# Pinning the sums of keys and values of batches 2 to 7 behind their neighbour in VectorE's queue

## The chip, the cores and the metric

The kernel runs on one core of one Trainium2 chip. The metric is the device time of one execution in microseconds (us). A core has a matrix engine (TensorE, PE in the profile, with its weight loads as PEld), VectorE (DVE), ScalarE (ACT), GpSimd (POOL) and SyncE (SP), whose queue issues the transfers between HBM and on-chip memory. Each engine has an instruction queue of its own.

## The reference

An attention with pooled keys and values feeds a dense feed-forward layer, whose output feeds a routed layer of eight experts. Cut to what matters here:

```python
# q, k, v: (8 batches, 8 heads, 576 tokens, 64)
k_p = k.reshape(B, H, 72, 8, D).mean(axis=3)      # mean over 8 neighbouring tokens
v_p = v.reshape(B, H, 72, 8, D).mean(axis=3)
attn = softmax(q @ k_p.transpose(0, 1, 3, 2) / sqrt(64))
x = (attn @ v_p) laid out as (4608 tokens, 512)
x2 = softplus(x @ w_in) @ w_out                   # 512 -> 2048 -> 512
out = top expert of 8 for each row of x2, weighted by its softmax probability
```

The change concerns how the means over 8 tokens (kept as sums; the factor is taken care of elsewhere) are placed among the other work.

## The kernel before

**Tiling.** The 4608 tokens are 12 blocks of 384. For each block the dense layer runs over 16 slices of the hidden width (`fc` 0 to 15): `mm1` makes a slice of the hidden layer on TensorE, `softplus` turns it on ScalarE and VectorE into `g`, `split_wo` prepares the second weights (ScalarE, then GpSimd or VectorE), and `mm2`, which trails `mm1` by two slices, adds into the block's four sums in PSUM. At a block's end `x2_out` copies the sums (ScalarE and VectorE) and stores them to HBM.

**Attention between the slices.** Block 0 and the attention that it needs are given first, by a list written out by hand (`ORDER`). From block 1 on there are two gaps per slice (lines 1033 to 1045), and `make_plan` (line 447) hands each gap its steps of attention: loading and transposing a tile of queries (`Q`), its scores and softmax (`S`), the transposes of the weights (`T`), the products with the values (`AV`), and the preparation of keys and values of batches 2 to 7. Of each such batch the plan gives, in this order: `FK`, the copies of keys from HBM (two of 512 KB, one of 128 KB); at least nine gaps later seven `PK` pieces (five sums of keys, `ks` four times and `klm` once, then two multiplications `km` on GpSimd, line 201); four `KT` pieces (the transposes of `km` and `klm` on TensorE, lines 252 and 255, and two copies to `kbd` on VectorE, lines 257 and 260); after the `PK` pieces `FV`, the copies of values (two of 512 KB and six of 64 KB); at least nine gaps later four `PV` and two `PR` pieces (six sums of values, `vs` four times and `vl` twice). `build_r` and `build_v` (lines 278 to 299) take the sums of values up when the previous batch's last `AV` is given.

**Buffers.** The copies of keys and values of these batches go into three buffers (pool `stp`, tag `st`). `FK` needs the buffers that the sums of values of the batch before have read, and `FV` those that the sums of keys of its own batch have read. All copies are issued from SP's queue.

**What sets the order.** TensorE's and SP's instructions stand in their queues as the program gives them (`manual_schedule`, line 997). For VectorE, ScalarE and GpSimd, behind the hand-written part, the compiler's scheduler chooses the order by a simulated timeline: an instruction whose inputs are there in that timeline may be placed ahead of ones given earlier.

**The sums.** A sum is one `tensor_reduce` over a 128 x 512 (or 96 x 512, 64 x 512) tile on VectorE: `pool_sum`, line 173, called by `add` (line 193) from `prep_k`, `prep_v` and `prep_r`. Steps named in `ALT` use three additions on GpSimd in its place; all of those belong to batches 0 and 1. The time-line and wait rows below name the sums by line 173, TensorE's scores by line 322, its second transposes of attention by line 393, its hidden layer and sums by lines 629 to 631, the router's product by line 709.

Of the kernel before, what the change touches and what calls it, by code (L numbers as in the profile page):

```python
# [13 lines left out]
ALU = mybir.AluOpType  # L14
AX = mybir.AxisListType
# [5 lines left out]
def tile_attention_moe_moe(  # L21
# [13 lines left out]
    nc = tc.nc  # L35
    P = 128
    B, H, S, D = q.shape
    POOL = 8
# [130 lines left out]
            nc.sync.dma_start(qt[p0:p0 + n], q[b, :, s:s + n, :].rearrange("h s d -> s h d"))  # L169
        q_t[t] = qt  # L170

    def pool_sum(dst, src):
        nc.vector.tensor_reduce(dst, src.rearrange("p (e d) -> p d e", e=POOL), AX.X, ALU.add)

    def rows(a, b):
        return a[b].rearrange("h (s e) d -> (h s) (e d)", e=POOL)
# [7 lines left out]
    def tree_sum(dst, src):  # L184
        nc.gpsimd.tensor_tensor(src[:, 0:4 * D], src[:, 0:4 * D], src[:, 4 * D:], ALU.add)
        nc.gpsimd.tensor_tensor(src[:, 0:2 * D], src[:, 0:2 * D], src[:, 2 * D:4 * D], ALU.add)
        nc.gpsimd.tensor_tensor(dst, src[:, 0:D], src[:, D:2 * D], ALU.add)


    def alt(step):  # L190
        return step in ALT

    def add(dst, src, step):
        (tree_sum if alt(step) else pool_sum)(dst, src)


    def times(dst, src, by, b, eng):
# [36 lines left out]
    def prep_k(b):  # L234
        ks = kp.tile([P, NJ, D], F32, tag="ks", name=f"ks{b}")
        for j in range(NJ):
            add(ks[:, j, :], st_t["k", b, j // 2][:, j % 2, :], f"K{b}.s{j}")
            yield
        add(klm[:, 1, :], st_t["kl", b][0:64, :], f"K{b}.s4")
        yield  # L240
        km = tp.tile([P, NJ, 2, D], F32, tag="wf", bufs=2, name=f"km{b}")
        km_t[b] = km
        for hh in range(2):
            times(km[:, :, hh, :], ks, hm[:, hh:hh + 1], b, "V" if alt(f"K{b}.m{hh}") != (hh == 1) else "A")
            yield
# [18 lines left out]
    def prep_v(b):  # L264
        vs = kp.tile([P, NJ, D], F32, tag="vs", name=f"vs{b}")
        kv_t[b] = vs
        for j in range(NJ):
            add(vs[:, j, :], st_t["v", b, j // 2][:, j % 2, :], f"V{b}.s{j}")
            yield
# [842 lines left out]
```

## Time and profile before

| | |
|---|---|
| median of three runs | 1480.05 us (1479.39 to 1480.74) |
| the profiled execution | 1478.74 us, its span 1476.9 us |
| TensorE busy over the span | 1396.5 us (95%) |
| VectorE, ScalarE, GpSimd busy | 781.4, 741.5, 330.0 us |
| mean granted clock of TensorE | 0.977 of full speed |
| sums by line 173 | 75, of 1.0 to 1.1 us each |

All times inside a run are microseconds from the start of the span of the profiled execution. A row of a time line gives the start, the duration, the engine, the line, the operation, what is written and read with its sizes, and in square brackets how long the engine was idle before it and what ended that. Durations of the queue's own instructions (SPq) are those of issuing, not of the transfer.

### The profile page before, as it was taken

How to read it: one execution, taken by the hardware profiler on the slowest of the kernel's cores; microseconds unless marked ns; L12 is line 12 of the kernel's file. 1: busy time of each engine (PE TensorE's matmuls, PEld its weight loads, DVE VectorE, ACT ScalarE, POOL GpSimd, SP SyncE). 2: the span in 40 equal slices, each digit the busy share in tenths (PEclk: the TensorE clock that was granted, in tenths of full speed). 3: DMA queues.
4: the chain of work that ended last, by engine and by line, in shares of the span. 5: the costliest groups of instructions: out<-in, count | busy, mean ns of one | idle time of the engine just before them, and what ended most of it. 6: DMA issues, size and time to landing. Idle time of an engine off the chain costs nothing.

```text
span 1476.9 us, 20327 instructions
## 1 busy us (share of the span) xinstructions
PE 1396.5 (95%) x7810; PEld 1315.9 (89%) x7810; DVE 781.4 (53%) x1599; ACT 741.5 (50%) x1593; POOL 330.0 (22%) x305
## 2 busy tenths in 40 slices
PE   5778989899988999998899999999999999999998
PEld 5667979798988999898899999999989999999997
DVE  6989876677566566656556564645513111111111
ACT  4776756466664666666466666767621111111111
POOL 5853432223122131312222121214200000000000
PEclk8889999999998999999999999999999999999999
DMA  7552411113021030302102010105123211111101
GB/s 236 182 167 72 144 39 47 58 47 97 8 83 47 1 97 8 97 8 82 47 1 65 1 51 1 43 1 185 58 107 87 85 65 64 65 64 65 64 22 44
DMA packets 71379, 99.92 MB, mean 68 GB/s; under 512 B 40040, under 2 KB 50280, under 8 KB 68208
## 3 DMA queue, kind: packets, MB, share of 16 engines
q1 hardware_dynamic: 71280, 98.60, 20.4%
q8 instruction: 63, 1.03, 0.3%
q14 instruction: 36, 0.29, 0.1%
HBM read 70.27 MB, written 28.31 MB: 67 GB/s over the span
## 4 chain that ended last, share of the span: by engine, by line
PE 75%; DVE 10%; DMA 7%; ACT 3%; SPq 2%; issue 1%; POOL 1%; DVEq 0%; ACTq 0%; POOLq 0%
PE h L629 11%; PE h L631 11%; PE h L630 11%; PE acc L629 7%; PE acc L631 7%; PE acc L630 7%; PE y L630 5%; PE y L631 5%; DMA st<-in_v_dram 5%; PE y L629 4%; PE pp L322 2%; DMA q<-in_q_dram 1%; DVE g L661 1%; SPq L230 1%; PE lg L709 1%
## 5 line engine op out<-in xcount | busy, mean ns | idle before, releaser
L629 PE MATMUL h<-xT,wi 128*128 128x384 f32 x768 | 265.7, 346 | 6.6 <-DVE t L657 5.9
L630 PE MATMUL h<-xT,wi 128*128 128x384 f32 x768 | 260.2, 339 | 2.2 <-DVE xT L431 2.1
L629 PE MATMUL acc<-g,wo 128*128 128x384 f32 x748 | 259.0, 346 | 2.8 <-ACT sq L699 2.8
L631 PE MATMUL h<-xT,wi 128*128 128x384 f32 x768 | 259.8, 338 | 0.0
L630 PE MATMUL acc<-g,wo 128*128 128x384 f32 x748 | 251.8, 337 | 0.8 <-DVE g L661 0.8
L631 PE MATMUL acc<-g,wo 128*128 128x384 f32 x748 | 252.0, 337 | 0.0
L621 POOL TENSOR_TENSOR wo<-wof,wo 128x512 fp32r<-128x512 f32 x95 | 125.0, 1316 | 443.5 <-ACT wo L617 443.4
L826 DVE SCALAR_TENSOR_TENSOR h<-h,h 128x384 fp32r<-128x384 f32 x96 | 53.5, 557 | 311.1 <-ACT h L825 311.1
L825 ACT ACTIVATE h<-h 128x384 fp32r<-128x384 f32 x96 | 47.2, 492 | 323.5 <-PE h L631 323.5
L661 DVE TENSOR_TENSOR g<-t,g 128x384 fp32r<-128x384 f32 x187 | 146.7, 784 | 51.0 <-ACT g L659 50.3
L657 DVE SCALAR_TENSOR_TENSOR t<-h,t 128x384 f32<-128x384 f32 x187 | 103.5, 553 | 132.0 <-ACT t L649 130.0
L645 ACT ACTIVATE t<-h 128x384 f32<-128x384 f32 x192 | 94.0, 490 | 147.4 <-PE h L631 146.8
L629 PEld LDWEIGHTS h<-xT,wi 128*128 128x128 f32 x768 | 146.8, 191 | 9.2 <-DVE t L657 6.8
L617 ACT CAST wo<-wof 128x512 fp32r<-128x512 f32 x187 | 116.2, 621 | 72.0 <-PE acc L631 69.7
L630 PEld LDWEIGHTS h<-xT,wi 128*128 128x128 f32 x768 | 146.6, 191 | 3.4 <-DVE xT L431 3.1
L629 PEld LDWEIGHTS acc<-g,wo 128*128 128x128 f32 x748 | 141.5, 189 | 7.7 <-ACT sq L699 5.7
L631 PEld LDWEIGHTS h<-xT,wi 128*128 128x128 f32 x768 | 146.4, 191 | 0.0
L630 PEld LDWEIGHTS acc<-g,wo 128*128 128x128 f32 x748 | 141.5, 189 | 1.6 <-DVE g L661 1.3
L631 PEld LDWEIGHTS acc<-g,wo 128*128 128x128 f32 x748 | 141.3, 189 | 0.0
L659 ACT CAST g<-t 128x384 fp32r<-128x384 f32 x187 | 96.0, 513 | 73.9 <-DVE t L657 73.4
L631 PE MATMUL h<-x2T,w 128*128 128x384 f32 x384 | 129.5, 337 | 0.0
L629 PE MATMUL h<-x2T,w 128*128 128x384 f32 x384 | 129.3, 337 | 0.0
(193 smaller groups left out, 2485.2 us busy)
## 6 DMA issues: line engine op xcount, KB each, us to landing
x2s<-x SPq DMA_DIRECT2D x12, 1536.0 KB
x2T<-x2s SPq DMA_DIRECT2D x12, 1536.0 KB
out_dram<-o SPq DMA_DIRECT2D x36, 256.0 KB
st<-in_k_dram SPq DMA_DIRECT2D x16, 512.0 KB
q<-in_q_dram SPq DMA_DIRECT2D x32, 256.0 KB
st<-in_v_dram SPq DMA_DIRECT2D x16, 512.0 KB
st<-in_moe_w_in_dram SPq DMA_DIRECT2D x16, 512.0 KB
st<-in_moe_w_out_dram SPq DMA_DIRECT2D x16, 512.0 KB
```

The lines of the kernel that those rows point to most:

```text
L322: nc.tensor.matmul(pp[p0:p0 + n, i, :], qT[:, j, p0:p0 + n], kbd_t[b][:, j, :], start=True, stop=True)
L617: nc.scalar.copy(w[:, 0, :], wof[:, fc, :])
L621: eng.tensor_tensor(w[:, 1, :], wof[:, fc, :], f32(w)[:, 0, :], ALU.subtract)
L629: nc.tensor.matmul(ps, ll, rh, start=first, stop=False)
L630: nc.tensor.matmul(ps, lh, rl, start=False, stop=False)
L631: nc.tensor.matmul(ps, lh, rh, start=False, stop=last)
L645: nc.scalar.activation(t, h, AF.Abs)
L657: nc.vector.scalar_tensor_tensor(t, h, 0.0, t, ALU.max, ALU.add)
L659: nc.scalar.copy(g[:, 0, :], t)
L661: nc.vector.tensor_tensor(g[:, 1, :], t, f32(g)[:, 0, :], ALU.subtract)
L825: nc.scalar.activation(g[:, 0, :], h, AF.Relu)
L826: nc.vector.scalar_tensor_tensor(g[:, 1, :], h, 0.0, f32(g)[:, 0, :], ALU.max, ALU.subtract)
```

## The change

`pool_sum` takes a third argument. For batches 2 to 7 it is true, and the sum is handed to `keep_in_program_order`, which adds one edge of order, without a wait for completion, from the instruction that was given last on the same engine to the sum. The sum can then not be placed ahead of that one instruction. Nothing keeps that neighbour from being moved, and instructions given after the sum may still be placed ahead of it. `add` reads the batch's number out of the step's name ("K5.s2" is batch 5). Instructions, sizes, buffers and the program's own order are the same.

```diff
-    def pool_sum(dst, src):
-        nc.vector.tensor_reduce(dst, src.rearrange("p (e d) -> p d e", e=POOL), AX.X, ALU.add)
+    def pool_sum(dst, src, pin):
+        ins = nc.vector.tensor_reduce(dst, src.rearrange("p (e d) -> p d e", e=POOL), AX.X, ALU.add)
+        if pin:
+            tc.keep_in_program_order(ins)
...
     def add(dst, src, step):
-        (tree_sum if alt(step) else pool_sum)(dst, src)
+        if alt(step):
+            tree_sum(dst, src)
+        else:
+            pool_sum(dst, src, int(step[1:step.index(".")]) > 1)
```

## Rows read from the trace of the kernel before

**Rows 1.** The page's first part: busy time of each engine, share of the span, instructions.

```profile
PE 1396.5 (95%) x7810; PEld 1315.9 (89%) x7810; DVE 781.4 (53%) x1599; ACT 741.5 (50%) x1593; POOL 330.0 (22%) x305
```

**Rows 2.** The waits of TensorE between 150 and 1000 us: what waited, for what, us in total, times, longest; the two largest.

```profile
PE pp L322 <- DVE aL L399: 10.6, 2, 5.4
PE pl L393 <- DVE xT L431: 9.0, 3, 4.8
```

**Rows 3.** TensorE's time line at its eight idle times of over 1 us between 150 and 1000 us.

```profile
190.12 0.85 PE L709 MATMUL lg<-x,eT 128*32 128x384 f32 x2 [3.68 <-DVE kbd L257]
...
273.52 0.85 PE L322 MATMUL pp<-kbd,qT 128*128 128x144 f32 x2 [5.69 <-DVE kbd L257]
...
364.75 0.44 PE L629 MATMUL h<-xT,wi 128*128 128x384 f32 x1 [1.97 <-DVE t L657]
...
441.43 0.42 PE L393 MATMUL pl<-ident,el 128*96 128x128 f32 x2 [3.73 <-DVE xT L431]
...
476.09 1.33 PE L322 MATMUL pp<-kbd,qT 128*128 128x144 f32 x4 [5.45 <-DVE aL L399]
...
618.11 0.45 PE L629 MATMUL h<-xT,wi 128*128 128x384 f32 x1 [2.10 <-DVE t L657]
...
695.87 0.66 PE L393 MATMUL pl<-ident,el 128*96 128x128 f32 x2 [4.83 <-DVE xT L431]
...
731.45 0.85 PE L322 MATMUL pp<-kbd,qT 128*128 128x144 f32 x2 [5.16 <-DVE aL L399]
```

**Rows 4.** Windows at the six stretches of lower clock between 150 and 1000 us, and one of the same length right behind one of them: the stretch, its length, then busy time and count of PE, PEld, DVE, ACT and POOL, the granted clock, the share of the DMA engines, GB/s.

```profile
189.94:193.35 3.41, 3.23 (x11) 1.78 (x12) 3.41 (x8) 1.95 (x4) 2.08 (x1) 0.50 0.12 37
271.86:278.69 6.83, 5.17 (x17) 4.74 (x17) 4.90 (x10) 1.61 (x3) 2.66 (x3) 0.50 0.00 1
442.53:445.94 3.41, 3.41 (x13) 3.41 (x12) 1.95 (x5) 1.55 (x3) 0.12 (x1) 0.50 0.02 5
473.25:480.08 6.83, 3.99 (x14) 4.00 (x15) 5.20 (x10) 0.51 (x1) 1.18 (x2) 0.50 0.01 4
695.11:701.94 6.83, 6.07 (x20) 6.06 (x21) 3.81 (x8) 1.91 (x4) 1.95 (x3) 0.50 0.00 0
729.25:736.08 6.83, 4.63 (x16) 4.64 (x17) 5.20 (x10) 0.51 (x1) 1.18 (x2) 0.50 0.00 0
480.08:483.49 3.41, 3.41 (x21) 3.41 (x21) 0.99 (x3) 2.01 (x5) 0.00 (x0) 1.00 0.00 0
```

**Rows 5.** Windows with line 173 alone: the stretch, its length, VectorE's busy time in sums and their count, clock, DMA share, GB/s. The first holds the sums of values of batch 5, the second the sums of keys of batch 6.

```profile
466.00:476.00 10.00, 6.12 (x6) 0.86 0.11 42
545.00:552.00 7.00, 5.27 (x5) 1.00 0.29 106
```

**Rows 6.** VectorE's time line in two of the bursts of sums (keys of batch 5, values of batch 5), and, in the last two rows, the view of line 173: us and times that VectorE sat idle ahead of a sum until a copy landed, over the whole run.

```profile
440.03 1.01 DVE L173 TENSOR_REDUCE klm<-st 64x64 f32<-64x512 f32 x1
440.97 0.41 DVE L431 TENSOR_TENSOR xT<-pv,xT 128x256 fp32r<-128x256 f32 x1
...
466.11 1.07 DVE L173 TENSOR_REDUCE vs<-st 128x64 f32<-128x512 f32 x1 [2.13 <-DMA st<-in_v_dram]
...
474.43 1.01 DVE L173 TENSOR_REDUCE vl<-st 96x64 f32<-96x512 f32 x1 [2.27 <-DMA st<-in_v_dram]
475.35 0.68 DVE L399 TENSOR_TENSOR aL<-pm,aH 128x512 fp32r<-128x512 f32 x1
...
  DMA st<-in_v_dram: 18.0, 9
  DMA st<-in_k_dram: 6.6, 5
```

**Rows 7.** VectorE's time line at five instructions that the program gives right ahead of a sum: of the third and fourth sum of keys of batch 2, of the fourth of batch 3, of the second of batch 5, of the last (`klm`) of batch 5, and of the first sum of values of batch 5.

```profile
174.41 0.69 DVE L621 TENSOR_TENSOR wo<-wof,wo 128x512 fp32r<-128x512 f32 x1
...
255.74 0.42 DVE L431 TENSOR_TENSOR xT<-pv,xT 128x256 fp32r<-128x256 f32 x1 [0.41 <-ACT xT L429]
...
479.16 0.55 DVE L661 TENSOR_TENSOR g<-t,g 128x384 fp32r<-128x384 f32 x1
...
489.31 0.55 DVE L661 TENSOR_TENSOR g<-t,g 128x384 fp32r<-128x384 f32 x1
...
519.76 0.68 DVE L621 TENSOR_TENSOR wo<-wof,wo 128x512 fp32r<-128x512 f32 x1
```

**Rows 8.** TensorE's time line at the first transposes of the keys of batches 2, 3 and 5 (line 252), and, last, the view of line 201: the multiplications of keys on GpSimd, with least, median and greatest duration in ns, first and last start.

```profile
180.78 0.60 PE L252 MATMUL pk<-ident,km 128*128 128x128 f32 x4
...
266.74 0.49 PE L252 MATMUL pk<-ident,km 128*128 128x128 f32 x3
...
507.21 0.38 PE L252 MATMUL pk<-ident,km 128*128 128x128 f32 x2
...
L201 POOL TENSOR_SCALAR km<-ks,hm x12: 922/960/1438, 156.6 to 695.2; 128x256 f32<-128x256 f32 x12
```

**Rows 9.** Transfers. SP's time line at the six small copies of values of batch 5 (one row for the six); then two pieces of the chain of work that ended last, in order of time (start, us, what): the landing of the last of these copies, and that of a tile of queries; then TensorE's time line at the tile of queries whose load stands in SP's queue right behind the copies of values of batch 2.

```profile
462.19 3.99 SPq L230 DMA_DIRECT2D st<-in_v_dram  x6
...
465.58 8.77 DMA st<-in_v_dram
...
167.83 9.42 DMA q<-in_q_dram
...
230.32 0.49 PE L305 MATMUL pq<-ident,q 128*128 128x128 f32 x3
```

## The prediction

> **What bounds the kernel now.** I read the page's busy times first. TensorE is busy 95% of the span, VectorE 53% [rows 1], so TensorE sets the end, and what can be won is its idle time and its time at a lower clock. Next the waits of TensorE, between 150 and 1000 us, where the pinned sums lie: the largest end at VectorE [rows 2]. Its time line then gives the places: eight idle times of 3.68, 5.69, 1.97, 3.73, 5.45, 2.10, 4.83 and 5.16 us, 32.6 us together [rows 3]. The next question is what VectorE was doing just before each. Values of batch 5 show it: six sums stand in one burst, 6.1 us of work in 10 us [rows 5], the queue stands still 2.13 and 2.27 us for copies that have not landed, and the aL that TensorE waits for starts only when the last sum is out of the way, at 475.35 [rows 6]; TensorE starts at 476.09. With keys of batch 5 the same: the sums end at 441.0, and xT, which TensorE wants at 441.43, starts at 440.97 [rows 3, 6]. In the other six the sequence is the same: a burst of line 173 ends, what TensorE waits for follows it. So the sums were placed far ahead of their turn, in one run each, and the queue behind them pays.
>
> The last view is the granted clock. [...] At 0.50 it gets through 13 instructions in 3.41 us of full work, at 1.00 through 21, close to half [rows 4].
>
> **The change part by part.** It removes and adds no instruction. It moves 66 sums (five of keys and six of values in each of six batches) back behind the instruction given just ahead of each.
>
> *How far they move.* Each neighbour can be found in the trace by counting the instructions of its line. The second sum of keys of batch 5 has its neighbour at 479.16 and klm at 489.31 [rows 7], where today the burst ends with klm at 440.03 [rows 6]; the first sum of values of batch 5, today at 466.11, has it at 519.76 [rows 6, 7]. So these move some 50 us back, and the plan's pieces put one or two sums in a gap and not six in a run.
>
> *What goes away: waits of VectorE for copies.* VectorE idles 18.0 us for values and 6.6 us for keys ahead of sums over the run [rows 6]. With the moved sums a copy must land later to be late. The last six copies of values of batch 5 could be issued only when klm has been summed (their buffer): 489.31 + 0.55 + 1.05 = 490.9; six issues take 3.99 us and the last lands 8.77 us after its issue [rows 7, 9], so all is there by 503.7, and the first sum stands behind 519.76. 16 us are spare, and I put these waits at nothing from batch 2 on.
>
> *What goes away: idle time of TensorE.* All eight idle times end behind a burst [rows 3], so I take off the whole 32.6 us.
>
> *What goes away: the lower clock.* A stretch at 0.50 costs half of the time that TensorE works in it. Of the six, it works 3.23, 5.17, 3.41, 3.99, 6.07 and 4.63 us [rows 4], together 26.5, so 13.2 us come back if no idle time takes their place.
>
> *What it may add: keys too late.* The transposes of keys stand in TensorE's queue, which waits in order, so a late sum stops it. Batch 2 is tightest: the neighbour ends at 175.1, two sums (2.1 us) and two multiplications on GpSimd (0.96 each) give 179.1, the transposes come at 180.78 [rows 7, 8]: 1.7 us spare. Batch 3: 256.2 + 1.05 + 1.9 = 259.1 against 266.74, 7.6 us spare; batch 5: the fourth sum has the same neighbour as the third, an instruction before 479.16, so the multiplications end by about 484 against 507.21 [rows 7, 8]. Bounds for batch 2: nothing, or about 2 us if its klm, behind a chain of other work, comes a sum late. I take 0.5 us.
>
> *What it may add: SP's queue.* The copies of values now wait for the last sum of keys at its later place, and the loads of queries queue behind them. In batch 2 the last sum of keys stands close to the transposes at 180.78 [rows 8]; with some microseconds of delay and 4 us of issues the copies are out by about 190, the next tile of queries lands 9.42 us after its issue, near 200, and TensorE wants it at 230.32 [rows 9]. I put this at nothing; with that cover gone it would cost what the load is late.
>
> *What it may add: each sum delays its surroundings by 1.05 us.* 66 sums make 70 us, all at new places. The nearest row: the five sums of keys of batch 6 in a burst, with 5.27 us of work at 545 to 552 [rows 5], are followed by no idle time of TensorE [rows 3]. If five in a row pass unseen, one or two mostly will too. The lower bound is a small gain (VectorE has less in front of it elsewhere), say -1.5 us; the upper, if one sum in three met a deadline with no slack, is 22 x 1.05 = 23 us. I take 3 us, near the lower end, because of that row.
>
> *What is late next.* With the eight gone, TensorE's own work is the limit: in the stretch right behind the burst of batch 5 it is busy 3.41 of 3.41 us at full clock [rows 4].
>
> The sum, against the profiled execution: 1478.74 - 32.6 - 13.2 + 0.5 + 3 = 1436.4. The median of the runs lies 1.31 us above the profiled one, so 1437.7, rounded to 1438.
>
> **The rivals.**
>
> *Half comes back (chance 0.18).* The sums sit at better places, but where a gap holds two of them beside attention steps, VectorE still hands over late, and some idle times of 3 us or more pull the clock down again. For it: 70 us of sums must go somewhere, and the aL or xT that TensorE waits for has little slack [rows 3]. Against it: the burst of batch 6 [rows 5]. Half of 45.8 us: about 1457.
>
> *Nothing comes of it (0.05).* The edge binds a sum to one neighbour alone. If the scheduler moves the neighbours forward as well, the bursts stay, and the time stays at 1480. Against it: such neighbours, an xT behind ScalarE by 0.41 us, a wo, a g [rows 7], have inputs that are not there early. The same time would follow if busy shares decided: VectorE is busy 53% [rows 1], so relief on it would be worth nothing. [...] The rows do not bear that reading out here: TensorE's idle times end at VectorE [rows 2].
>
> *Slower (0.07).* A pinned sum now waits for its copy with all of VectorE behind it. The place is the ring of three buffers: values are fetched when the keys' sums are done, the next keys when the values' sums are done, both now later. Its price from the burst of batch 5: VectorE held 4.4 us by two waits and 6.1 us by sums cost TensorE 5.45 us [rows 3, 5, 6], so about 5 us of a hold pass unseen. If each of the 12 groups held VectorE 10 us, TensorE would lose 5 us twelve times and 2.2 us of clock each time (13.2 over six), 86 us against the 45.8 won: about 1520. It decides from some 7 us of hold per group on, at which copies would have to land over 20 us later than I reckon, given the 16 us spare. [...]
>
> **How the numbers follow.** The forecast has 0.70, half back 0.18, nothing 0.05, slower 0.07. The lower end is the sum with no cost for late keys and the -1.5 us: 1478.74 - 45.8 - 1.5 + 1.31 = 1432.8; a microsecond more for the spread of runs, 1431. The upper end takes in most of the half-back case, 1458; what lies above it is about 0.2. Faster by over 0.2% (3 us, about what a measurement of this kernel can tell from no change): 0.88, within it 0.05, slower 0.07.
>
> **What would show it.** In the changed kernel's time line the sums stand singly or in pairs, those of values of batch 5 behind a time of about 510 us; idle ahead of line 173 for copies is near nothing after 150 us; the eight idle times of TensorE are gone and its clock stays at 1.00 from 150 to 1000 us. The first 145 us and everything from the experts on stay as they are. The prediction is wrong if TensorE's waits at lines 252 or 255 (late keys), at 305 (late queries) or at 322 and 393 (VectorE late again) appear in their place.

## The result and the profile after

The changed kernel takes 1431.08 us (median of four, 1430.42 to 1431.41) against 1479.72 for the kernel before on the same chip: a ratio of 0.967, 95% interval 0.966 to 0.969, or 48.6 us. The span of the profiled execution falls from 1476.9 to 1429.7 us. In the rows below the lines of the changed kernel count seven higher than before (the scores are line 329, aL 406, xT 438); the sum is line 175.

The page's first part and its row of the granted clock, which answer to [rows 1]:

```profile
PE 1384.9 (97%) x7810; PEld 1307.8 (91%) x7810; DVE 783.3 (55%) x1599; ACT 743.6 (52%) x1593; POOL 330.5 (23%) x305
...
PEclk8889999999999999999999999999999999999999
```

VectorE's busy time is as before (783.3 against 781.4 us). TensorE is idle for 1429.7 - 1384.9 = 44.8 us where it was idle for 80.4, which is 35.6 us less, and its own work takes 11.6 us less, since less of it runs at the lower clock (mean granted clock 0.977 before, 0.986 after). The two make up the 47.2 us of the span. The same two between 150 and 1000 us, in the window view of each kernel (columns as in [rows 4]), first before, then after:

```profile
150.00:1000.00 850.00, 813.24 (x4823) 790.07 (x4822) 534.03 (x1128) 530.41 (x1154) 215.78 (x187) 0.98 0.15 46
```

```profile
150.00:1000.00 850.00, 845.87 (x5089) 824.15 (x5088) 563.57 (x1180) 567.87 (x1227) 235.25 (x202) 1.00 0.19 57
```

The idle time, the length less PE's busy time, has gone from 36.8 to 4.1 us, and the clock is 1.00 throughout. All that is left of TensorE's waits there, against [rows 2]:

```profile
PE acc L636 <- ACT sq L706: 2.4, 6, 0.6
PE pl L400 <- DVE xT L438: 0.6, 1, 0.6
PE pp L329 <- DVE kbd L264: 0.3, 1, 0.3
PE pk L262 <- DVE kbd L264: 0.2, 1, 0.2
```

Of the eight places of [rows 3] one is left, with 0.29 us in place of 5.69: the scores that wait for kbd at batch 3. VectorE's time line shows where the six sums of values of batch 5 stand now, against the burst of [rows 5, 6]:

```profile
490.51 0.68 DVE L628 TENSOR_TENSOR wo<-wof,wo 128x512 fp32r<-128x512 f32 x1
491.11 1.09 DVE L175 TENSOR_REDUCE vs<-st 128x64 f32<-128x512 f32 x1
...
498.91 1.07 DVE L175 TENSOR_REDUCE vs<-st 128x64 f32<-128x512 f32 x1
...
500.97 1.07 DVE L175 TENSOR_REDUCE vs<-st 128x64 f32<-128x512 f32 x1
...
509.35 1.07 DVE L175 TENSOR_REDUCE vl<-st 96x64 f32<-96x512 f32 x1
...
510.81 1.07 DVE L175 TENSOR_REDUCE vs<-st 128x64 f32<-128x512 f32 x1
511.81 1.05 DVE L175 TENSOR_REDUCE vl<-st 96x64 f32<-96x512 f32 x1
```

The reader is to see three things: the first sum stands right behind its neighbour wo, the six are spread over 22 us and not 9, and no bracket tells of a wait for a copy. The view of line 175 says the same for the whole run; the 3.0 us left lie in the first 12 us, and the wait for values has no row any more:

```profile
  DMA st<-in_k_dram: 3.0, 3
```

### The profile page after: what moved, and what is told of

Its sections match the earlier page's. It is cut to its first block, busy times and chain, and to the rows that moved or that the text cites. A ratio compares the mean times of both kernels' runs of the same rounds, so it can differ in the third digit from the quotient of the medians.

```text
span 1429.7 us, 20346 instructions
## 1 busy us (share of the span) xinstructions
PE 1384.9 (97%) x7810; PEld 1307.8 (91%) x7810; DVE 783.3 (55%) x1599; ACT 743.6 (52%) x1593; POOL 330.5 (23%) x305
## 4 chain that ended last, share of the span: by engine, by line
PE 84%; DVE 8%; ACT 3%; DMA 2%; issue 1%; POOL 1%; SPq 0%; DVEq 0%; ACTq 0%; POOLq 0%
PE h L636 13%; PE h L638 13%; PE h L637 13%; PE acc L636 8%; PE acc L637 8%; PE acc L638 8%; PE y L637 5%; PE y L638 5%; PE y L636 5%; PE pp L329 2%; DVE g L668 1%; PE lg L716 1%; DMA q<-in_q_dram 1%; PE pq L312 1%; DVE wof L614 1%
## 5 line engine op out<-in xcount | busy, mean ns | idle before, releaser
L832 ACT ACTIVATE h<-h 128x384 fp32r<-128x384 f32 x96 | 47.2, 492 | 323.5 <-PE h L638 323.5
L636 PEld LDWEIGHTS h<-xT,wi 128*128 128x128 f32 x768 | 144.8, 189 | 3.8 <-DVE t L664 2.1
L637 PEld LDWEIGHTS h<-xT,wi 128*128 128x128 f32 x768 | 144.7, 188 | 2.6 <-DVE xT L438 2.3
L638 PEld LDWEIGHTS h<-xT,wi 128*128 128x128 f32 x768 | 144.4, 188 | 0.0
L638 PE MATMUL h<-x2T,w 128*128 128x384 f32 x384 | 129.5, 337 | 0.0
L636 PE MATMUL h<-x2T,w 128*128 128x384 f32 x384 | 129.3, 337 | 0.0
L637 PE MATMUL h<-x2T,w 128*128 128x384 f32 x384 | 128.9, 336 | 0.0
```

The costliest lines, as they stand in the source:

```text
L636: nc.tensor.matmul(ps, ll, rh, start=first, stop=False)
L637: nc.tensor.matmul(ps, lh, rl, start=False, stop=False)
L638: nc.tensor.matmul(ps, lh, rh, start=False, stop=last)
L832: nc.scalar.activation(g[:, 0, :], h, AF.Relu)
```

## The experiments

Each was timed in three rounds beside the kernel before on the same chip (1477.8 to 1480.1 us there); the ratios are to that kernel. Where a run is set against the changed kernel, the two medians can come from different chips, on which the kernel before alone differs by 2.3 us; a difference of that size says nothing.

**Keys alone, values alone.** The condition in `add` asks for one kind of sum as well.

```diff
-            pool_sum(dst, src, int(step[1:step.index(".")]) > 1)
+            pool_sum(dst, src, int(step[1:step.index(".")]) > 1 and step[0] == "K")    # run 1
+            pool_sum(dst, src, int(step[1:step.index(".")]) > 1 and step[0] != "K")    # run 2
```

> Only the 30 sums of keys of batches 2 to 7 are pinned; the 36 sums of values may float. Theory A (a burst of early sums holds VectorE by its waits for copies and by its own work together; TensorE pays what goes beyond some 5 us, and half of the time that it then works at the lower clock): the bursts of values stay, and with them idle times of about 24 us and 8.5 us of clock, so about 1431 + 32 = 1463 us (1452 to 1470). Theory B (only VectorE's waits for copies cost, not the work in the burst): values carry 18.0 of 24.6 us of those waits, so about 1431 + 0.75 x 49 = 1467. Theory C (the gain comes from copies being issued at other times): keys' pins alone delay the copies of values, so most of the gain is there, 1435 to 1445.

> Only the 36 sums of values are pinned; the sums of keys may float. Theory A: the two bursts of keys that stopped TensorE (batches 5 and 7: 3.73 and 4.83 us, and 4.7 us of clock) stay, about 1431 + 13 = 1444 us (1436 to 1448). Theory B: keys carry 6.6 of 24.6 us of the waits, about 1431 + 13 = 1444 as well; but the idle times would follow the waits, so batch 6 (2.75 us of wait) would stop TensorE before batch 5 (none). Theory C: the copies of keys come later, those of values do not, so about half of the gain, 1455.

Keys alone: 1470.98 us, ratio 0.994 (0.992 to 0.996). Values alone: 1454.36 us, 0.983 (0.981 to 0.986). The first speaks against theory C: the pins of keys alone bring little, though they delay the copies of values. The second came out at C's 1455, so C is taken up again below. Both runs lie above theory A's ranges, by 1 and 6 us, and the two gains, 9 and 25 us, don't add up to 48.6. With keys alone the values' idle times moved and grew. VectorE's time line in batch 4 of that run:

```profile
369.46 2.05 DVE L175 TENSOR_REDUCE vs<-st 128x64 f32<-128x512 f32 x2
373.34 1.01 DVE L175 TENSOR_REDUCE vl<-st 96x64 f32<-96x512 f32 x1 [1.83 <-DMA st<-in_v_dram]
...
377.11 1.01 DVE L175 TENSOR_REDUCE vl<-st 96x64 f32<-96x512 f32 x1 [2.30 <-DMA st<-in_v_dram]
...
379.67 0.29 DVE L438 TENSOR_TENSOR xT<-pv,xT 128x128 fp32r<-128x128 f32 x1 [0.33 <-ACT xT L436]
```

TensorE's time line, where it takes that xT up:

```profile
380.11 0.60 PE L421 MATMUL pv<-aH,VL 128*128 128x320 f32 x1 [6.57 <-DVE xT L438]
```

The floating sums of values now run into the pinned sums of keys and then wait for copies that were issued later than before: the six small ones of batch 4 at 366.64, right behind its first two sums of values (364.56 to 366.62), where it was 348.64, 7 us ahead of the burst. VectorE's wait for values is 23.8 us in all, where it was 18.0. With values alone the two idle times of keys stood where theory A had them, batches 5 and 7:

```profile
431.96 0.66 PE L400 MATMUL pl<-ident,el 128*96 128x128 f32 x2 [3.77 <-DVE xT L438]
...
678.60 0.66 PE L400 MATMUL pl<-ident,el 128*96 128x128 f32 x2 [4.86 <-DVE xT L438]
```

Batch 6 has none, though its first sum of keys waited 3.09 us for its copy (2.75 in the kernel before). So for keys the wait is not what counts. Two more idle times, of 2.20 and 1.86 us, came up at 215 and 316 us, where floating sums of keys stand between the pinned sums of values of the batch before; they are part of what lies above theory A's range.

**Short sums, floating.** In the kernel before:

```diff
-        nc.vector.tensor_reduce(dst, src.rearrange("p (e d) -> p d e", e=POOL), AX.X, ALU.add)
+        nc.vector.tensor_reduce(dst, src[:, 0:n * D].rearrange("p (e d) -> p d e", e=n), AX.X, ALU.add)
...
+            pool_sum(dst, src, 1 if int(step[1:step.index(".")]) > 1 else POOL)
```

> The kernel before with nothing pinned, but each sum of keys or values of batches 2 to 7 adds up one token of eight in place of eight (seven eighths of the sum are left out), so that it takes about 0.2 us in place of 1.05; the copies are whole. Theory A: a burst then holds VectorE by its waits (2 to 4.4 us) and about 1.2 us of work, hardly beyond 5 us: 1431 to 1440 us. Theory B: the waits for copies are all there still, and so is nearly all of the idle time: 1470 to 1480 us. Theory C: copies are issued as before: 1470 to 1480 us.

1473.32 us, 0.995 (0.993 to 0.997): theory A, which my prediction rested on, does not hold as a whole here, and the time lies where theories B and C had it. A sum took 0.2 us and the idle time at values of batch 5 was still 4.78 us (TensorE's time line):

```profile
473.24 1.09 PE L325 MATMUL pp<-kbd,qT 128*128 128x144 f32 x3 [4.78 <-DVE aL L402]
```

VectorE's time line shows why:

```profile
468.48 0.22 DVE L173 TENSOR_REDUCE vl<-st 96x64 f32<-96x64 f32 x1 [3.09 <-DMA st<-in_v_dram]
468.62 0.54 DVE L664 TENSOR_TENSOR g<-t,g 128x384 fp32r<-128x384 f32 x1
472.37 0.22 DVE L173 TENSOR_REDUCE vl<-st 96x64 f32<-96x64 f32 x1 [3.21 <-DMA st<-in_v_dram]
472.51 0.68 DVE L402 TENSOR_TENSOR aL<-pm,aH 128x512 fp32r<-128x512 f32 x1
```

What the sums saved, the waits took back: the last row of values still comes when its copy has landed, and aL behind it. Over the run VectorE's wait for values rose from 18.0 to 43.0 us:

```profile
  DMA st<-in_v_dram: 43.0, 19
  DMA st<-in_k_dram: 13.9, 12
```

At the keys the shorter work did count: TensorE's two idle times there fell to 0.86 and 1.19 us (from 3.73 and 4.83):

```profile
440.83 0.42 PE L396 MATMUL pl<-ident,el 128*96 128x128 f32 x2 [0.86 <-DVE xT L434]
...
693.64 0.42 PE L396 MATMUL pl<-ident,el 128*96 128x128 f32 x2 [1.19 <-DVE xT L434]
```

So theory D: a burst of values holds VectorE until the last small copy has landed, even with sums of 0.2 us; a burst of keys, whose copies mostly were there, by its work.

**Without the small copies, floating, with whole and with short sums.** Two runs on the kernel before.

```diff
     def fetch_vl(b, g):
+        if b >= 2:
+            st_t["vl", b, g] = st_t["v", b, 1][:, g, :]
+            return
```

> The kernel before, nothing pinned, without the six small copies of values per batch for batches 2 to 7; the two vl sums read rows of the second large copy in their place (so these two sums are of other rows). New theory D, after the short floating sums: in a burst of values VectorE is held until the last small copy has landed, however long the sums take, while in a burst of keys the work of five sums counts. D: bursts of values end 2 to 4 us sooner, their idle times shrink from 24 to about 9 us and their clock loss from 8.5 to about 4, the two idle times of keys stay (13 us with the clock): about 1457 us (1450 to 1465). If the small copies don't matter: 1475 to 1482.

> As the run without small copies, still floating, and each sum of batches 2 to 7 adds up one token of eight (seven eighths left out). Theory D: with neither the late landing nor the work, both kinds of burst pass nearly unseen although the sums are as early as before: 1431 to 1442 us. If the large copies' landing holds VectorE just as long, or if it is the early place by itself: 1460 us or more.

With whole sums 1459.96 us, 0.987 (0.985 to 0.990); with short sums 1431.67 us, 0.969 (0.966 to 0.971). Both as theory D says. In the first, aL of batch 5 follows the sums without a wait between, and TensorE's idle time there is 2.95 us, not 5.45 (VectorE's time line, then TensorE's):

```profile
458.95 2.06 DVE L173 TENSOR_REDUCE vs<-st 128x64 f32<-128x512 f32 x2
460.92 1.98 DVE L173 TENSOR_REDUCE vl<-st 96x64 f32<-96x512 f32 x2
463.26 0.69 DVE L402 TENSOR_TENSOR aL<-pm,aH 128x512 fp32r<-128x512 f32 x1
```

```profile
464.01 0.61 PE L325 MATMUL pp<-kbd,qT 128*128 128x144 f32 x1 [2.95 <-DVE aL L402]
```

At batch 3 no sum of values waited for a copy in this run, and TensorE was idle for 3.08 us all the same (5.69 before). So theory B is out for values too: with the small copies gone, it is the work of the sums that holds VectorE.

In the second the sums are as early as ever and unpinned, and still TensorE waits for next to nothing between 150 and 1000 us:

```profile
PE pl L399 <- DVE xT L437: 2.9, 3, 1.5
PE acc L635 <- ACT sq L705: 2.5, 6, 0.6
PE pp L328 <- ACT qT L314: 0.4, 1, 0.4
PE pp L328 <- DVE kbd L263: 0.3, 1, 0.3
```

The early place itself therefore costs next to nothing. What costs is that it puts the late landing and the work of a whole group in front of one deadline of TensorE. Taking away one of the two leaves part of the loss, since the other still holds VectorE; taking both away in place of pinning gives the changed kernel's time within 0.6 us (2.2 by the ratios). It also settles theory C: the large copies of values of batch 5 were issued at 437.54, 30 us behind the store of x2s at 407.53. In the kernel before that distance was 34 us (426.57 and 461.02), in the changed one 42 (410.63 and 452.55). The whole gain is there without later copies.

**The last two sums of values alone.** `step[0] == "R"` in the condition.

> Only the twelve vl sums (the last two of each batch's sums of values, the second of which waited 2.1 to 2.6 us for its copy) are pinned. Theory A: each burst of values loses that wait and two sums, about 4.4 us of hold; of their idle times at most 1 to 2 us are left, the bursts of keys stay with 13 us: 1444 to 1450 us. Theory B: 14 of some 20 us of waits behind 150 us are gone, so 0.7 of the gain: about 1445 us too; but what is left would follow the waits that are left (values of batches 5 and 7, keys of batch 6) and not the bursts of keys of batches 5 and 7.

1460.70 us, 0.987 (0.984 to 0.990), over 10 us above either expectation. Idle times of 2.84 and 2.68 us stayed at values of batches 5 and 7 and of 3.73 and 4.63 at keys of batches 5 and 7, and the mean granted clock between 150 and 1000 us was 0.98, where the changed kernel has 1.00. That the keys' idle times stay with batches 5 and 7, not 6, speaks against theory B once more; the size of what is left I had put too low. It is nearly what the run without small copies left: 2.95 and 2.74 us at values of batches 5 and 7, 3.73 and 4.63 at keys, 1459.96 us in all. Here the copies were all made and the sums whole, which speaks for the late landing ahead of TensorE's deadline as what counted there, and against the traffic of the small copies.

**Sums done twice.** In the changed kernel, first all 66 pinned ones, then those of batches 4 to 7.

```diff
             tc.keep_in_program_order(ins)
+            ins = nc.vector.tensor_reduce(dst, src.rearrange("p (e d) -> p d e", e=POOL), AX.X, ALU.add)
+            tc.keep_in_program_order(ins)
```

> The changed kernel with every pinned sum done twice, one behind the other: 66 more instructions of about 1.05 us, 69 us more of VectorE's time. Theory A: single sums at their places pass unseen, and two behind one another mostly too: 1431 to 1437 us. Rival D (sums at their new places use up slack that TensorE needs; my upper bound of 23 us for the first 66): the second 66 cost 15 to 30 us and pull the clock down: 1446 to 1465 us.

> The changed kernel with the pinned sums of batches 4 to 7 alone done twice (44 of 66). In the run with all of them doubled, TensorE's idle times over 1 us all lay in batches 2 and 3, where the plan puts two sums in a gap and keys close to their transposes. If that is where it costs: within 3 us of the changed kernel, 1429 to 1435 us. If each doubled sum costs alike (19 us over 66): about 1444 us.

All of them twice: 1449.97 us, 0.980 (0.978 to 0.981), 19 us above the changed kernel, which by itself is what rival D gave (D of that expectation, not theory D). The largest part is one place, keys of batch 2, on TensorE's time line; the other two rows shown are at values of batch 2:

```profile
186.06 1.12 PE L261 MATMUL pk<-ident,km 128*128 128x128 f32 x4 [6.70 <-POOL km L210]
...
219.80 0.38 PE L423 MATMUL pv<-aH,VL 128*128 128x256 f32 x1 [1.53 <-DVE xT L440]
...
224.42 0.42 PE L402 MATMUL pl<-ident,el 128*96 128x128 f32 x2 [1.33 <-DVE xT L440]
```

Batches 4 to 7 alone: 1433.65 us, 0.970 (0.968 to 0.972). 44 more sums, of 1.0 to 1.1 us each, cost 2.6 us (4.3 by the ratios). So the cost is not spread over the sums. All of TensorE's idle times over 0.75 us in the run with all sums doubled lie before 325 us, in batches 2 and 3. There the plan differs from later batches: in batch 2 it puts two sums in a gap, and in batches 2 and 3 the transposes of keys come within a gap of the last piece of their preparation, where from batch 4 on they come four gaps later.

**Pins for batches 4 to 7 alone.** `> 3` for `> 1`.

> Only the sums of batches 4 to 7 are pinned. If the prices of the bursts add up: the two idle times of batches 2 and 3 (3.68 and 5.69 us) and their clock (4.2 us) stay, about 1431 + 14 = 1445 us (1440 to 1449). If pins of one group move others to worse places, as with keys alone: above 1452.

1443.39 us, 0.976 (0.974 to 0.979). The idle times of batches 2 and 3 are back, nearly to the tenth of a microsecond, in the waits of TensorE:

```profile
PE pp L329 <- DVE kbd L264: 5.7, 1, 5.7
PE lg L716 <- DVE kbd L264: 3.6, 1, 3.6
```

9.3 us of idle time, and with it a mean granted clock of 0.984 in place of 0.986, make up most of the 12.3 us that this run lies above the changed kernel. By batches the prices add up; by keys and values they don't. The copies that went out 18 us later with keys alone, behind sums of values, point to the ring of buffers that the two share as the reason; no run separates it.

**A lead of one gap.** `LEAD = 1` for 9 in the changed kernel.

> The changed kernel with the plan's least distance from a fetch to its first sum cut from nine gaps to one. Copies can then land after their sum's turn, and a pinned sum holds all of VectorE until they do. The slower rival's price (TensorE loses what goes beyond some 5 us of hold, and 2.2 us of clock for each longer stop): holds of 3 to 10 us in most of the twelve groups, 1440 to 1500 us. If copies are issued so far ahead of their place in the program that they are there all the same: within 5 us of 1431.

1441.89 us, 0.974 (0.972 to 0.976): neither of the two. The lead got shorter for keys above all: by the plan's rule, which also looks for free gaps, their first sum comes one or two gaps behind the fetch, that of values four to eight (before: nine or ten, but six in batch 2, where I wrote nine for all). No pinned sum waited for a copy (3 waits of 2.9 us, all ahead of 150 us), so no wait of that kind is behind the 10.8 us. TensorE has 10 us of idle time in seven pieces of 0.75 to 3.38 us; the mean granted clock was 0.988, against 0.986 in the changed kernel. The largest piece is in batch 2, where the sums of keys now fall among the copies at the end of block 0: TensorE waited for an `e` that GpSimd took up at 170.30, right behind the two multiplications of keys (168.51 to 170.33). The other pieces I did not take apart.

## Why the prediction was right

The forecast was 1438 us in a range from 1431 to 1458; 1431.1 is at its lower end, inside by 0.1 us.

*The sums move and the waits for copies go.* As forecast, though the first sum of values of batch 5 stands at 491.1 and not near 510: all before it had become faster too. The last six copies of that batch were issued from 462.28 on, SP's time line:

```profile
462.28 4.01 SPq L237 DMA_DIRECT2D st<-in_v_dram  x6
```

With the landing of [rows 9] they were there by about 475, 16 us ahead of the first sum of values.

*Idle time and clock.* The term of 32.6 us held: idle time between 150 and 1000 us fell from 36.8 to 4.1, which is 32.7. The term of 13.2 us for the clock held there as well, with 1.00 in place of 0.98: behind 150 us TensorE's busy time fell by 13.9 us. In the kernel before the six stretches at 0.50 begin during the six idle times of 3.68 to 5.69 us or, once, 1.1 us behind one [rows 3, 4]; at the two of 1.97 and 2.10 us (windows 360 to 368.2 and 617 to 621) the clock was 1.00. The reason given for the half was weak, since 13 instructions against 21 are 0.62 and not close to half, and the two stretches hold other shapes. Products of one shape bear the half out: in the kernel before those of the hidden layer start 0.32 us apart from 479.13 to 480.09, at 0.50, and 0.17 us apart behind it, at 1.00. In the first 150 us the clock was a little lower than before in the profiled execution, 0.87 against 0.90, with 2.3 us more of busy time, and idle time fell by 2.9 us outside of the stretch.

*Keys too late.* I had reckoned 1.7 us to spare in batch 2. The time lines of VectorE, GpSimd and TensorE show almost none:

```profile
175.43 2.07 DVE L175 TENSOR_REDUCE ks<-st 128x64 f32<-128x512 f32 x2
```

```profile
177.60 2.08 POOL L208 TENSOR_SCALAR km<-ks,hm 128x256 f32<-128x256 f32 x2 [5.94 <-DVE ks L175]
```

```profile
179.73 0.66 PE L259 MATMUL pk<-ident,km 128*128 128x128 f32 x4
```

The multiplications end at 179.68, 0.6 us later than reckoned, and the transposes start at 179.73, 1.0 us earlier than in the kernel before. It cost nothing as it stood, and 6.70 us as soon as the sums were doubled.

*The terms that were mis-sized.* The 3 us for sums among other work and the 0.5 us for late keys did not show: the 44 doubled sums put the price of one more sum in batches 4 to 7 at 2.6 / 44 = 0.06 us (0.1 by the ratios). Without these two terms the sum would have been 1434. Of the 3 us left, 1.4 are the span's (47.2 against 45.8); the rest is the distance from the profiled execution to the median, 1.3 us upwards before and 0.3 us downwards now.

*The reason that failed in part.* I wrote that a burst costs by its waits and its work together, and that some 5 us of a hold pass unseen. For values that is not so: the short sums changed the time by 6 us only, since a burst ends with the landing of its last copy, and the work counts only once that landing is gone. The slower rival's price rests on the same sum of waits and work and falls with it. Its condition did not come about either, and not for keys with a lead of one or two gaps: in that run the copies of keys of batch 5 were issued at 417.00, 16 us ahead of the first sum at 432.93, though two gaps are about 5 us (32 gaps, one block, take 82 us there: the stores of x2s start at 416.59 and 498.26). Whether values with so short a lead would hold VectorE stays open. "Half comes back" and "nothing comes of it" are out by the waits above.

## What to carry to other kernels

A scheduler that lets an instruction go as soon as its simulated input has landed can put a whole group in front of one deadline. Here the group also stood behind copies that had not landed on the chip; when the simulation had them landed is not on record. The sign in a profile is a pair of rows: the idle bracket of the engine that sets the end names another engine, and that engine's time line shows a run of one line with waits for copies in it. Pin such instructions to where their results are wanted, all kinds that share buffers together (here 9 and 25 us apart, 48.6 together), and leave room ahead of the first use, since that is where the price came back here (6.70 us at keys of batch 2 with the sums doubled).

## What was not expected of the hardware

Shortening 66 sums that follow transfers from 1.05 to 0.2 us each gave 6 us of 1480 (VectorE's busy time fell by 49), and VectorE's idle time for values rose by 25.0 us instead. How busy VectorE is said nothing of its part in the time: it worked 781 us before and 783 after, and 48.6 us lay between.
